# Loading the last eighth of an output projection on half of the DMA engines: a study of one change to a decode-attention kernel

## The chip, the cores and the metric

One core of one Trainium2 chip. The metric is device time of one execution in microseconds; every row of times below is a median over executions. Every experiment was timed in the same rounds, on the same chip, as the kernel before. Different experiments ran on three different chips, so kernels are compared by their ratios to the kernel before, with a 95% interval; a difference of 1% is 2 us here.

## The reference

```python
B, Sq, D = 32, 1, 512            # x
Hq, Hkv, Sk, Dh = 32, 8, 2048, 128
W = max(256, Sk // 4)            # 512: only the last 512 cache rows count
q = (x @ wq) -> [B, Hq, 1, Dh]
scores = q . k[:, :, Sk-W:] * Dh**-0.5;  p = softmax(scores);  o = p . v[:, :, Sk-W:]
return o.reshape(B, 1, Hq*Dh) @ wo       # wo: [4096, 512] bf16
```

The last line is what matters here. Its contraction runs over 4096 rows of `wo`, 4 MB in bf16, which the kernel reads after the caches.

## The kernel before: the parts concerned

`wo` is read in eight eighths of 512 rows. Partition m holds four consecutive rows (4 KB) of each eighth. The contraction therefore needs attention outputs arranged by "row 4m + i", while they lie in `oT_sb` by head and channel; a **selection** moves them: matmuls of `oT_sb` with a 0/1 matrix `band`, then copies into `o_sel`. The first selection takes batches 0 to 27 while the last P·V products still run, the second the last four.

```python
for hg in range(NHG):                                   # NHG = 8, SyncE's queue
    sp.dma_start(wo_sb[:, hg]..., wo[hg*512:(hg+1)*512, :].rearrange("(m i) n -> m (i n)", i=4)
    ).then_inc(sem_wo[hg], 16)
...
def select(b0, b1, dst):                                # TensorE
    pe.wait_ge(dve_oT, b1)
    for i in range(4):
        for hi in range(4):
            ins = pe.matmul(dst(i), lhsT=band[:, i, 96-32*hi:224-32*hi],
                rhs=oT_sb[:, :, b0:b1].rearrange("p (g hi) b -> p hi g b", hi=4)[:, hi], ...)
    ins.then_inc(pe_sel, 1)
...
for it in range(B + PVLAG):                             # PVLAG = 6
    if it < B: transposes(it)
    if 1 <= it <= B: scores(it - 1)
    if it >= PVLAG: pv_matmuls(it - PVLAG)
    if it % 4 == 1 and 5 <= it <= B + 1: pt_transposes((it - 5) // 4)
    if it == SELCUT + PVLAG: ...; select(0, SELCUT, ...)   # SELCUT = 28
select(SELCUT, B, ...)
pe.wait_ge(dve_sel, 2); pe.wait_ge(act_sel, 1)
for hg in range(NHG):                                   # the projection
    pe.wait_ge(sem_wo[hg], 16)
    for i in range(4):
        for c in range(4):
            ins = pe.matmul(KT_ps[:, 2, :].bitcast(F32)[32*c:32*(c+1), 0:128],
                lhsT=o_sel[:, i, hg, :], rhs=wo_sb[:, hg, i, c*128:(c+1)*128], ..., tile_position=(0, 32*c))
```

Of the kernel before, what the change touches and what calls it, by code (L numbers as in the profile page):

```python
# [5 lines left out]
BF16 = mybir.dt.bfloat16  # L6
# [6 lines left out]
def bass_standalone__sliding_block_cached__sampling_kernel(  # L13
# [27 lines left out]
    LEAD = 5  # L41
    PVLAG = 6
    NQUAD = B // 4
    NHG = HQ // 4
    SELCUT = 28

    with ExitStack() as es:  # L47
# [1 line left out]
        ps = lambda name, shape, dt: es.enter_context(nc.psum_tensor(name, shape, dt))  # L49
        sem = lambda name: es.enter_context(nc.semaphore(name))  # L50

        w_sb = sb("w_sb", [P, DKT * HD], BF16)
        wq_sb = w_sb[:, :].rearrange("p (kt n) -> p kt n", kt=DKT)
        wo_sb = w_sb[:, :].rearrange("p (g i n) -> p g i n", g=NHG, i=4)
        K_sb = sb("K_sb", [P, NK, 2, NR, DH], BF16)
        V_sb = sb("V_sb", [P, NV, 2, NR, DH], BF16)
        KT_sb = sb("KT_sb", [P, NKT, 2, NR, G4, NS], BF16)
# [4 lines left out]
        PT_sb = sb("PT_sb", [P, 2, NR, P], BF16)  # L62
        oT_sb = sb("oT_sb", [P, HQ, B], BF16)
        o_sel = sb("o_sel", [P, 4, NHG, B], BF16)
        band = sb("band", [P, 4, 224], BF16)
        xT_sb = sb("xT_sb", [P, DKT, 32], BF16)
        ident = sb("ident", [P, P], BF16)
        perm = sb("perm", [P, G4, NS], BF16)
# [13 lines left out]
        sem_x = sem("sem_x")  # L82
        sem_wq = [sem(f"sem_wq{i}") for i in range(DKT)]
        sem_wo = [sem(f"sem_wo{i}") for i in range(NHG)]
        sem_k = [[sem(f"sem_k{i}_{h}") for h in range(2)] for i in range(NK)]
        sem_v = [sem(f"sem_v{i}") for i in range(NV)]
        sem_out = sem("sem_out")
# [39 lines left out]
        @block.sync  # L127
        def _(sp):
            for kt in range(1, DKT):
                sp.dma_start(wq_sb[:, kt, :], wq[kt * P:(kt + 1) * P, :]).then_inc(sem_wq[kt], 16)  # L130

            def load_k(b):
                if b >= NK:
                    sp.wait_ge(pe_T[3], b - NK + 1)
                for h in range(2):
                    sp.dma_start(  # L136
                        K_sb[:, b % NK, h].rearrange("p r d -> p (r d)"), cache_rows(k_cache, b, h)
                    ).then_inc(sem_k[b % NK][h], 16)

            def load_v(b):  # L140
                if b >= NV:
                    sp.wait_ge(pe_PV, b - NV + 1)
                for h in range(2):
                    sp.dma_start(  # L144
                        V_sb[:, b % NV, h].rearrange("p r d -> p (r d)"), cache_rows(v_cache, b, h)
                    ).then_inc(sem_v[b % NV], 16)

            for b in range(B + LEAD):
                if b < B:
                    load_k(b)  # L150
                if b >= LEAD:
                    load_v(b - LEAD)
            sp.wait_ge(pe_qt, 1)
            for hg in range(NHG):
                sp.dma_start(  # L155
                    wo_sb[:, hg].rearrange("p i n -> p (i n)"),
                    wo[hg * 512:(hg + 1) * 512, :].rearrange("(m i) n -> m (i n)", i=4),
                ).then_inc(sem_wo[hg], 16)
            sp.wait_ge(dve_out, 2)
            sp.wait_ge(act_out, 2)  # L160
            sp.dma_start(
                out.rearrange("b s n -> b (s n)"), out_sb[:, :, :].rearrange("b c n -> b (c n)")
            ).then_inc(sem_out, 16)
            sp.wait_ge(sem_out, 16)

        @block.gpsimd
        def _(pool):
            pool.memset(ident[:, :], 0.0).then_inc(pool_init, 1)
            pool.wait_ge(pool_init, 1)
            pool.affine_select(  # L170
                out=ident[:, :], in_=ident[:, :], compare_op=ALU.not_equal, fill=1.0,
                base=0, pattern=[[-1, P]], channel_multiplier=1,
            ).then_inc(pool_init, 1)
            pool.memset(perm[:, :, :], 0.0).then_inc(pool_perm, 1)
            pool.wait_ge(pool_perm, 1)
            pool.affine_select(
                out=perm[:, :, :], in_=perm[:, :, :], compare_op=ALU.not_equal, fill=1.0,
                base=0, pattern=[[-1, G4], [-G4, NS]], channel_multiplier=1,
            ).then_inc(pool_perm, 1)
            pool.memset(junk[:, :], 0.0).then_inc(pool_init, 1)  # L180
            pool.memset(QBD[:, :, :, :], 0.0).then_inc(pool_init, 1)
            pool.memset(P_ex[:, :, :, :], 0.0).then_inc(pool_ex, 1)
            pool.memset(band[:, :, :], 0.0).then_inc(pool_band, 1)
            pool.wait_ge(pool_band, 1)
            pool.affine_select(
                out=band[:, :, :], in_=band[:, :, :], compare_op=ALU.not_equal, fill=1.0,
                base=384, pattern=[[-1, 4], [-4, 224]], channel_multiplier=1,
            ).then_inc(pool_band, 1)
            pool.wait_ge(pool_init, 4)
            pool.wait_ge(dve_qt, 1)  # L190
            pool.wait_ge(act_qt, 1)
            for b in range(B):
                if b >= NQB:
                    pool.wait_ge(pe_S, b - NQB + 1)
                dst = bass.AP(
                    tensor=QBD, offset=(b % NQB) * G * 32 + score_row(0, b % 4),
                    ap=[[NQB * G * 32, P], [G4 * 32 + 16, 2], [32, G4], [1, REP]],
                )
                src = bass.AP(
                    tensor=QT_sb, offset=b,  # L200
                    ap=[[HQ * B, P], [G4 * REP * B, 2], [REP * B, G4], [B, REP]],
                )
                pool.tensor_copy(dst, src).then_inc(pool_qbd, 1)  # L203

        @block.tensor
        def _(pe):
# [91 lines left out]
                        )  # L298
                ins.then_inc(pe_PV, 1)

            def select(b0, b1, dst):
                pe.wait_ge(dve_oT, b1)
                for i in range(4):
                    for hi in range(4):
                        ins = pe.matmul(
                            dst(i),
                            lhsT=band[:, i, 96 - 32 * hi:224 - 32 * hi],
                            rhs=oT_sb[:, :, b0:b1].rearrange("p (g hi) b -> p hi g b", hi=4)[:, hi],
                            start=(hi == 0), stop=(hi == 3), tile_position=(0, 0), skip_group_check=True,
                        )  # L310
                ins.then_inc(pe_sel, 1)

            for it in range(B + PVLAG):
                if it < B:
                    transposes(it)
                if 1 <= it <= B:
                    scores(it - 1)
                if it >= PVLAG:
                    pv_matmuls(it - PVLAG)
                if it % 4 == 1 and 5 <= it <= B + 1:  # L320
                    pt_transposes((it - 5) // 4)
                if it == SELCUT + PVLAG:
                    pe.wait_ge(pool_band, 2)
                    pe.wait_ge(dve_T, 3 * B)
                    pe.wait_ge(act_T, B)
                    nb = SELCUT
                    select(0, nb, lambda i: KT_ps[:, i // 2, :].bitcast(F32)[
                        :, (i % 2) * NHG * nb:(i % 2 + 1) * NHG * nb])
            nl = B - SELCUT
            select(SELCUT, B, lambda i: KT_ps[:, 3, :].bitcast(F32)[:, i * NHG * nl:(i + 1) * NHG * nl])  # L330
            pe.wait_ge(dve_sel, 2)
            pe.wait_ge(act_sel, 1)
            for hg in range(NHG):
                pe.wait_ge(sem_wo[hg], 16)
                for i in range(4):
                    for c in range(4):
                        ins = pe.matmul(  # L337
                            KT_ps[:, 2, :].bitcast(F32)[32 * c:32 * (c + 1), 0:128],
                            lhsT=o_sel[:, i, hg, :],
                            rhs=wo_sb[:, hg, i, c * 128:(c + 1) * 128],  # L340
                            start=(hg == 0 and i == 0), stop=(hg == NHG - 1 and i == 3),
                            tile_position=(0, 32 * c),
                        )
            ins.then_inc(pe_fin, 1)

        @block.vector
        def _(dve):
# [40 lines left out]
            def sel_evac(bank, i0, ni, b0, b1):  # L388
# [3 lines left out]
                        "p (i g b) -> p i g b", i=ni, g=NHG),  # L392
                )

            def ot_evac(b):
                dve.wait_ge(pe_PV, b + 1)
                dve.tensor_copy(oT_sb[:, :, b], QO_ps[:, 0:HQ]).then_inc(dve_oT, 1)  # L397

            for it in range(B + PVLAG + 1):
# [4 lines left out]
                if it == SELCUT + PVLAG + 1:  # L404
                    dve.wait_ge(pe_sel, 1)
                    dve.tensor_copy(*sel_evac(0, 0, 2, 0, SELCUT)).then_inc(dve_sel, 1)
                if it % 4 == 1 and 5 <= it <= B + 1:
                    softmax_b((it - 5) // 4)
                if it < B:
# [3 lines left out]
                    softmax_a((it - 4) // 4)  # L413
            dve.wait_ge(pe_sel, 2)
            dve.tensor_copy(*sel_evac(3, 0, 4, SELCUT, B)).then_inc(dve_sel, 1)
            dve.wait_ge(pe_fin, 1)
            for c in range(2):
                dve.tensor_copy(  # L418
# [85 lines left out]
```

## Time and profile before

| | before |
|---|---|
| median of 3 executions (range) | 196.53 us (196.02 to 196.56) |
| traffic, mean rate | 75.97 MB, 390 GB/s |
| TensorE / VectorE / ScalarE busy | 74% / 52% / 30% |
| projection can start, ends | 186.78 us, 192.06 us |
| eighth 7 of wo complete | 191.61 us |

The kernel is a stream of transfers with everything else beside it. Two groups of the page concern the end; the columns are busy time, mean ns of one, idle time before, and what ended most of it:

```profile
L337 PE MATMUL KT_ps<-w_sb,o_sel 128*32 128x128 bf16 x128 | 3.8, 289 | 1.9 <-DMA w_sb<-in_wo_dram 1.5
...
w_sb<-in_wo_dram SPq DMA_DIRECT2D x8, 512.0 KB, 15.4
```

The projection costs TensorE 3.8 us and waits for wo; each eighth takes some 15 us from issue to landing. Transfers of this size complete every 1.28 us (the first completions of eighths 0 and 1 are at 177.18 and 178.46), so a dozen are in the queue with it. What stands at the end of the timeline is shown in the prediction.

### The profile page before, as it was taken

To read this page: it belongs to the slowest core of one execution; us is meant where nothing else is said; L and a number is where in the kernel's file an instruction comes from. 1 tells how busy PE (TensorE), PEld (TensorE's weight loads), DVE (VectorE), ACT (ScalarE), POOL (GpSimd) and SP (SyncE) were. 2 spreads that over 40 slices of the span, in tenths; PEclk is the share of its full clock that TensorE was granted. 3 is DMA by queue.
4 is the path that set the end of the run, shared out by engine and by line. 5 is a ranking of instruction groups with operands and counts; after the bars stand their busy time and mean duration, and the time that the engine had idled before them with its cause. 6 is when DMAs were issued, how large, how long until landed. Compare 5 with 4: busy or idle time off the path is not lost.

```text
span 194.7 us, 6153 instructions
## 1 busy us (share of the span) xinstructions
PE 144.0 (74%) x2724; PEld 114.9 (59%) x2724; DVE 102.1 (52%) x190; ACT 57.6 (30%) x70; POOL 15.0 (8%) x45
## 2 busy tenths in 40 slices
PE   0448995877897679749777988779776978937881
PEld 0337773755586567537555667557666667636760
DVE  0005778745684459533944587447943574670211
ACT  3001535622262126213252236204420352213101
POOL 8502000000020001000000000000000000000000
PEclk9999999999699978996999699979998887975558
DMA  5999999999999999999999999999999999999960
GB/s 204 426 420 406 412 405 411 407 410 407 409 407 407 408 408 410 407 407 410 407 407 410 409 407 407 410 406 408 408 406 411 405 410 405 412 405 412 406 251 31
DMA packets 20282, 75.97 MB, mean 390 GB/s; under 512 B 2272, under 2 KB 2336, under 8 KB 19744
## 3 DMA queue, kind: packets, MB, share of 16 engines
q1 hardware_dynamic: 20208, 75.54, 97.2%
q8 instruction: 22, 0.36, 0.8%
q10 hardware_dynamic: 48, 0.03, 0.1%
q14 instruction: 4, 0.03, 0.0%
HBM read 75.53 MB, written 0.03 MB: 388 GB/s over the span
## 4 chain that ended last, share of the span: by engine, by line
SPq 68%; DMA 23%; PE 5%; issue 3%; DVEq 0%; DVE 0%
SPq L144 37%; SPq L136 26%; DMA K_sb<-in_k_cache_dram 15%; DMA w_sb<-in_wo_dram 8%; SPq L155 5%; PE KT_ps L243 4%; SPq L130 1%; PE S_ps L260 1%; PE QO_ps L293 0%; PE KT_ps L337 0%; SPq L118 0%; DVEq L47 0%; DVE out_sb L418 0%
## 5 line engine op out<-in xcount | busy, mean ns | idle before, releaser
L243 PE MATMUL KT_ps<-perm,K_sb 128*128 128x128 bf16 x1024 | 75.2, 235 | 22.4 <-DMA K_sb<-in_k_cache_dram 22.2
L361 DVE COPY KT_sb<-KT_ps 128x1024 bf16<-128x1024 bf16 x96 | 63.6, 689 | 52.2 <-PE KT_ps L243 52.0
L243 PEld LDWEIGHTS KT_ps<-perm,K_sb 128*128 128x128 bf16 x1024 | 65.6, 106 | 30.0 <-DMA K_sb<-in_k_cache_dram 28.4
L435 ACT ACTIVATE KT_sb<-KT_ps 128x1024 bf16<-128x1024 bf16 x32 | 32.8, 1023 | 82.3 <-PE KT_ps L243 82.3
L293 PEld LDWEIGHTS QO_ps<-PT_sb,V_sb 128*128 128x128 bf16 x1024 | 28.3, 97 | 17.8 <-issue 13.5
L293 PE MATMUL QO_ps<-PT_sb,V_sb 128*128 128x16 bf16 x1024 | 31.1, 171 | 3.3 <-DMA V_sb<-in_v_cache_dram 1.3
L383 DVE TENSOR_SCALAR P_ex<-P_f,recip 32x512 bf16<-32x512 f32 x32 | 25.4, 793 | 1.2
L260 PE MATMUL S_ps<-KT_sb,QBD 128*32 128x512 bf16 x256 | 22.2, 428 | 0.0
L453 ACT ACTIVATE PT_sb<-PT_ps 128x1024 bf16<-128x1024 bf16 x16 | 15.5, 1021 | 19.4 <-PE PT_ps L275 19.4
L203 POOL COPY QBD<-QT_sb 128x32 bf16<-128x32 bf16 x32 | 8.5, 279 | 116.1 <-PE S_ps L260 108.1
L275 PE MATMUL PT_ps<-ident,P_ex 128*128 128x128 bf16 x128 | 9.4, 231 | 9.8 <-DVE P_ex L383 9.8
L275 PEld LDWEIGHTS PT_ps<-ident,P_ex 128*128 128x128 bf16 x128 | 7.9, 104 | 10.9 <-DVE P_ex L383 10.8
L397 DVE CAST oT_sb<-QO_ps 128x32 bf16<-128x32 f32 x32 | 9.3, 289 | 7.5 <-PE QO_ps L293 7.5
L221 PE MATMUL PT_ps<-xT_sb,w_sb 128*128 128x32 bf16 x128 | 4.1, 188 | 6.4 <-DMA w_sb<-in_wq_dram 6.4
L367 DVE TENSOR_REDUCE maxv<-S_ps 128x1 f32<-128x512 f32 x8 | 5.5, 691 | 5.4 <-PE S_ps L260 5.4
L221 PEld LDWEIGHTS PT_ps<-xT_sb,w_sb 128*128 128x128 bf16 x128 | 3.7, 104 | 6.8 <-DMA w_sb<-in_wq_dram 4.6
L443 ACT ACTIVATE P_f<-S_ps,negmax 128x512 f32<-128x512 f32 x8 | 5.5, 687 | 6.3 <-DVE negmax L369 6.3
L260 PEld LDWEIGHTS S_ps<-KT_sb,QBD 128*32 128x32 bf16 x256 | 3.9, 96 | 3.9 <-issue 1.4
L353 DVE CAST QT_sb<-PT_ps 128x512 bf16<-128x512 f32 x1 | 0.7, 691 | 10.3 <-PE PT_ps L221 10.3
L337 PE MATMUL KT_ps<-w_sb,o_sel 128*32 128x128 bf16 x128 | 3.8, 289 | 1.9 <-DMA w_sb<-in_wo_dram 1.5
L337 PEld LDWEIGHTS KT_ps<-w_sb,o_sel 128*32 128x32 bf16 x128 | 2.9, 131 | 2.7 <-DMA w_sb<-in_wo_dram 2.2
L427 ACT ACTIVATE QT_sb<-PT_ps 128x512 bf16<-128x512 f32 x1 | 0.6, 597 | 12.0 <-PE PT_ps L221 12.0
(28 smaller groups left out, 22.4 us busy)
## 6 DMA issues: line engine op xcount, KB each, us to landing
K_sb<-in_k_cache_dram SPq DMA_DIRECT2D x64, 512.0 KB, 15.6
V_sb<-in_v_cache_dram SPq DMA_DIRECT2D x64, 512.0 KB, 15.4
w_sb<-in_wq_dram SPq DMA_DIRECT2D x4, 1024.0 KB, 8.3
w_sb<-in_wo_dram SPq DMA_DIRECT2D x8, 512.0 KB, 15.4
x_sb<-in_x_dram ACTq DMA_DIRECT2D x1, 32.0 KB, 2.9
out_dram<-out_sb SPq DMA_DIRECT2D x1, 32.0 KB, 1.5
```

Of the source, the lines that this page charges most:

```text
L136: sp.dma_start(K_sb[:, b % NK, h].rearrange("p r d -> p (r d)"), cache_rows(k_cache, b, h)).then_inc(sem_k[b % NK][h], 16)
L144: sp.dma_start(V_sb[:, b % NV, h].rearrange("p r d -> p (r d)"), cache_rows(v_cache, b, h)).then_inc(sem_v[b % NV], 16)
L155: sp.dma_start(wo_sb[:, hg].rearrange("p i n -> p (i n)"), wo[hg * 512:(hg + 1) * 512, :].rearrange("(m i) n -> m (i n)", i=4),).then_inc( ...
L243: ins = pe.matmul(KT_ps[:, t, i * 128:(i + 1) * 128], lhsT=K_sb[:, b % NK, h, 8 * (t % 2) + i, :], rhs=perm[:, :, :], start=True, stop=Tru ...
L260: ins = pe.matmul(S_ps[32 * c:32 * c + 32, :], lhsT=QBD[:, b % NQB, g, :], rhs=KT_sb[:, b % NKT, h, :, c, :], start=(j == 0 and h == 0), s ...
L275: ins = pe.matmul(PT_ps[:, r // 8, (r % 8) * 128:(r % 8 + 1) * 128], lhsT=P_ex[:, r, :, :].rearrange("p s g -> p (s g)"), rhs=ident[:, :], ...
L293: ins = pe.matmul(QO_ps[:, 16 * h:16 * h + 16], lhsT=V_sb[:, b % NV, h, r, :], rhs=PT_sb[:, q % 2, r, :].rearrange("p (c n) -> p c n", c=G ...
L361: dve.tensor_copy(KT_sb[:, b % NKT, t // 2, 8 * (t % 2):8 * (t % 2) + 8, :, :], KT_ps[:, t, :]).then_inc(dve_T, 1)
L383: dve.tensor_scalar(P_ex[rows, :, :, c], P_f32[rows, :].rearrange("p (r s) -> p r s", r=NR), recip[rows, q:q + 1], None, op0=ALU.mult,).th ...
L397: dve.tensor_copy(oT_sb[:, :, b], QO_ps[:, 0:HQ]).then_inc(dve_oT, 1)
L435: act.activation(KT_sb[:, b % NKT, 1, 8:16, :, :], KT_ps[:, 3, :], ACTF.Copy).then_inc(act_T, 1)
L453: act.activation(PT_sb[:, q % 2, 8 * i:8 * i + 8, :].rearrange("p r n -> p (r n)"), PT_ps[:, i, :], ACTF.Copy,).then_inc(act_PT, 1)
```

## The change

Intent: in the end phase half of the DMA engines run dry early (of the sixteen completions of eighth 7, eight are in by 188.40 us, the last at 191.61). Give the last eighth of `wo` to engines that are done first: as eight transfers of eight rows, with 8 KB rows in partitions 0 to 63. That layout puts eight rows of wo on a partition instead of four, so it needs its own selection (`band8`, 64 columns of weights) and a contraction over 64 rows with eight steps.

```diff
-    NHG = HQ // 4
+    NHG = HQ // 4 - 1;  NTP = 64;  NTI = 8
+            for half in range(2):
+                for r in range(4):
+                    rows = slice(32 * half + r, 32 * half + 32, 4)
+                    sp.dma_start(wt_sb[rows]..., wo[NHG*512:, :].rearrange("(m i) n -> m (i n)", i=NTI)[rows]
+                    ).then_inc(sem_wt, 16)
...                                     # GpSimd: memset and affine_select of band8
-            def select(b0, b1, dst):
+            def select(b0, b1, dst, dst_t):
...
+                for i in range(NTI):
+                    for hi in range(4):
+                        ins = pe.matmul(dst_t(i), lhsT=band8[:, i, 48 - 16*hi:112 - 16*hi],
+                            rhs=oT_sb[:, 4 * NHG + hi, b0:b1], ...)
...                                     # VectorE: one more copy (into t_sel) after each selection
+            pe.wait_ge(sem_wt, 128)
+            for i in range(NTI):
+                for c in range(4):
+                    ins = pe.matmul(KT_ps[...], lhsT=t_sel[:, i, :], rhs=wt_sb[:, i, c*128:(c+1)*128],
+                        start=False, stop=(i == NTI - 1), tile_position=(0, 32*c))
```

## The prediction

> **What bounds the kernel now.** I read the page first: its slices, then its chain that ended last.

> ```profile
> DMA  5999999999999999999999999999999999999960
> GB/s 204 426 420 406 412 405 411 407 410 407 409 407 407 408 408 410 407 407 410 407 407 410 409 407 407 410 406 408 408 406 411 405 410 405 412 405 412 406 251 31
> ...
> SPq L144 37%; SPq L136 26%; DMA K_sb<-in_k_cache_dram 15%; DMA w_sb<-in_wo_dram 8%; SPq L155 5%; PE KT_ps L243 4%; SPq L130 1%; PE S_ps L260 1%; PE QO_ps L293 0%; PE KT_ps L337 0%; SPq L118 0%; DVEq L47 0%; DVE out_sb L418 0%
> ```

> The DMA engines are busy in 37 of 40 slices at some 408 GB/s, and the chain is nearly all transfers and their issue: 75 MB of traffic sets the time, and no engine's arithmetic does. The change moves the same bytes, so only the last ten microseconds can give or take. There the rate is 251, then 31 GB/s: in the last two slices most DMA engines have run out while a few still work. The timeline of the end:

> ```profile
> 178.59 3.15 PE L305 MATMUL KT_ps<-oT_sb,band 128*128 128x224 bf16 x16
> ...
> 185.79 0.61 PE L305 MATMUL KT_ps<-oT_sb,band 128*128 128x32 bf16 x16 [0.39 <-DVE oT_sb L397]
> 186.44 0.29 DVE L415 CAST o_sel<-KT_ps 128x128 bf16<-128x128 f32 x1 [0.70 <-PE KT_ps L305]
> 186.78 2.06 PEld L337 LDWEIGHTS KT_ps<-w_sb,o_sel 128*32 128x32 bf16 x80 [0.49 <-DVE o_sel L415]
> 186.78 3.00 PE L337 MATMUL KT_ps<-w_sb,o_sel 128*32 128x128 bf16 x96 [0.38 <-DVE o_sel L415]
> ...
> 190.41 0.41 PE L337 MATMUL KT_ps<-w_sb,o_sel 128*32 128x128 bf16 x16 [0.63 <-DMA w_sb<-in_wo_dram]
> ...
> 191.66 0.41 PE L337 MATMUL KT_ps<-w_sb,o_sel 128*32 128x128 bf16 x16 [0.83 <-DMA w_sb<-in_wo_dram]
> ```

> TensorE is ready for the output projection at 186.78, catches up with the first five eighths of wo near 189, and then waits for eighths 5, 6 and 7, which are complete at 189.12, 190.37 and 191.61. The kernel ends when eighth 7 has landed and its 16 matmuls are done. The slack is small: 2.4 us from TensorE being ready to its first wait.

> Why do the eighths land late? Each 128-row transfer leaves sixteen completions in the trace, one per DMA engine. For eighth 6 the first is at 184.82, the eighth at 187.20, the ninth at 187.91, the last at 190.37; for eighth 7: 186.09, 188.40, 189.15, 191.61. In the first K transfer the spread was 0.94 us. The offsets stay constant to 0.1 us over long stretches, then one completion steps back by about 1.5 us each time a 16 KB packet of another queue passes:

> ```profile
> q8 instruction: 22, 0.36, 0.8%
> ```

> The sequence of steps repeats after eight: the ninth and tenth packet hit completions that the first and second had already moved back, so I read that only eight of the sixteen engines carry these packets, and the other eight finish some 3 us earlier. I cannot see an engine's number in the trace.

> [...] The trace before has nothing but transfers over 16 engines (128 or 32 rows)[...]. [...] the P·V matmuls (128 columns of weights, 16 moving) follow each other every 26.7 ns[...]. Nothing before has 64 columns on one position.

> **The change, part by part.**

> Transfers. Removed: eighth 7 as one transfer, 8 packets of 4 KB (159 ns each) on each of 16 engines. Added: 8 transfers of 8 rows of 8 KB[...]. An 8 KB packet takes 309 ns (the wq rows), so 8 take 2.45 us, against 1.25 us for eighth 7. Issue: the shortest issues in the trace take 0.36 to 0.6 us, back-pressured ones 1.08; eight of them from 176.64 end between 180 and 185.5, early enough. If engines 0 to 7 are the eight that carry no instruction packets, they start the tail between 184.82 and 187.20 and finish by 187.20 + 2.45 = 189.65. Then the last landing is eighth 6 at 190.37 instead of eighth 7 at 191.61: 1.24 us earlier.

> The end of TensorE. From 190.41 the program still has 16 matmuls for eighth 6 and then 32 for the tail (64 rows deep, but the number of matmuls doubles from 16 to 32). Four column tiles take 55 ns at full clock and 107 ns at half clock, so 48 matmuls take 0.66 us (full) or 1.28 us (half), plus 0.22 us until the last one drains. The windows table says which clock holds:

> ```profile
> 178.50:185.80 7.30, 6.13 (x122) 5.28 (x119) 1.81 (x5) 0.54 (x1) 0.00 (x0) 0.50 1.03 407
> 185.80:190.00 4.20, 3.54 (x112) 2.90 (x112) 0.29 (x1) 0.00 (x0) 0.00 (x0) 0.50 0.53 212
> 190.00:192.20 2.20, 0.81 (x32) 0.47 (x32) 0.08 (x1) 0.09 (x1) 0.00 (x0) 0.98 0.13 45
> ```

> The seventh figure after the length (PEclk) is 0.50 until 190 and then 0.98. At full clock the end of TensorE would be 190.41 + 0.66 + 0.22 = 191.29 against 192.06 before: a gain of 0.77 us if nothing else moved.

> The added selection. TensorE works alone through 178.6 to 186.8, so what is added there delays the projection. First selection: 16 matmuls shrink from 224 to 196 columns, at 1.2 columns per ns: 16 × 28 / 1.2 = −0.37 us. Added are 32 with 64 columns of weights and 28 moving. [...] if they go like 128 columns do here, 27 ns, 0.86 us. Second selection: 16 matmuls from 32 to 28 columns, −0.05 us; 32 added with 4 moving columns, again 1.71 or 0.86 us. VectorE has one more copy after each: the 128x448 copy took 0.62 us and the 128x128 one 0.29, so about 0.39 us for 224 columns and 0.2 for 32; the first delays the next evacuation only slightly, the second lies wholly in the path. Sum to the start of the projection: (1.71 − 0.37 + 0.1) + (1.71 − 0.05) + 0.25 = 3.4 us, so about 190.2; with 27 ns each 1.7 us, about 188.5. The slack of 2.4 us is thus overdrawn in the first case: 144 matmuls from 190.2 at full clock take 2.0 + 0.22 us and end at 192.4, 0.35 us later than before. In the second case the data still set the end and 191.3 to 191.5 holds: −0.65 us. GpSimd's extra memset and select (0.84 and 0.95 us for the same 896 columns) end near 9.5, well ahead of 15.47 where it is next needed: nothing.

> **The rivals.** (1) The eight engines are the wrong ones, those with the instruction packets. Then the slowest reaches the end of eighth 6 at 190.37 and needs 2.45 us more: 192.85, plus 32 matmuls and drain, 0.66 us: 193.5, or +1.4 us. For it: the trace has no numbers of engines. [...] I give it 0.25. (2) The selection takes the place of the transfer: right engines, but TensorE is the bound at the end, +0.35 us; if the clock stays at half to the end, 144 matmuls take 3.85 us and it is +2 us. For it: the half clock[...]. Against it: the pitch of 26.7 ns at 128 columns. I give it 0.45, of which 0.1 for half clock. (3) The intended gain: right engines, short selection, −0.65 us, 0.30. (4) All 16 engines share the eight-row transfers after all; the landing is then as before, and the selection alone costs up to 0.4 us. This lies within the others.

> **Range and chances.** 0.25 × 1.4 + 0.35 × 0.35 + 0.10 × 2 + 0.30 × (−0.65) = +0.48 us; executions of the kernel before differ by 0.5 us. From 196.53 I predict 196.9 us, and 195.7 to 198.6 holds all but the worst mixtures. Two per cent is 3.9 us, more than any of these makes: within 2% 0.96, slower 0.03 (weights slower still at half clock together with wrong engines), faster 0.01.

> **What would show the steps right or wrong.** The tail's semaphore should show 64 increments right at issue and 64 with data[...]. The tail's last landing near 189.6 says right engines, near 193 wrong ones. The last landing of wo on the whole should be 190.4 in the first case. The mean pitch of the 32 added selection matmuls decides between 53 and 27 ns. The idle time of the tail's matmuls says what bounds: none before them means TensorE, one put down to the wo transfer means DMA. The prediction would be wrong if the steady stage changed its rate, or if issuing eight transfers held up earlier ones.

## The result, and the profile after

| | before | after |
|---|---|---|
| median (range), 4 executions each | 196.41 us (196.02 to 196.56) | 198.38 us (197.82 to 198.63) |
| ratio | | 1.0099, interval 1.0073 to 1.0126 |
| first selection starts | 178.59 us | 177.90 us |
| projection starts | 186.78 us | 189.53 us |
| last landing of wo | 191.61 us | 190.89 us |
| projection ends | 192.06 us | 193.66 us |

A ratio here is the mean time of one kernel's executions over that of the other's of the same rounds, so not quite the ratio of the medians. The change is 1% slower: within 2%, but clear of noise. The two lines of the page that answer to those of before:

```profile
DMA  5999999999999999999999999999999999999930
GB/s 214 426 415 409 408 407 407 411 407 411 405 412 405 410 408 406 409 409 409 407 409 405 410 407 407 412 405 407 410 407 410 407 411 405 407 410 407 392 153 7
...
SPq 54%; DMA 24%; PE 14%; DVE 3%; issue 3%; ACT 1%; DVEq 0%; ACTq 0%
```

The last two slices move 153 and 7 GB/s instead of 251 and 31, but a slice is a fortieth of the span, so in the longer run these two begin some 1.5 us later. In the same stretch, 189.5 to 193.4, it is 13 GB/s instead of 40 (last figures of the windows below): the transfers do end somewhat earlier. In the chain that ended last TensorE now has 14% and VectorE 3%, where TensorE had 5%. The end in the timeline:

```profile
177.90 2.77 PE L324 MATMUL KT_ps<-oT_sb,band 128*128 128x196 bf16 x16
...
180.60 1.89 PE L332 MATMUL KT_ps<-oT_sb,band 128*64 128x28 bf16 x32
...
187.20 1.87 PE L332 MATMUL KT_ps<-oT_sb,band 128*64 128x4 bf16 x32
189.11 0.27 DVE L462 CAST o_sel<-KT_ps 128x112 bf16<-128x112 f32 x1 [2.50 <-PE KT_ps L332]
189.30 0.17 DVE L463 CAST t_sel<-KT_ps 64x32 bf16<-64x32 f32 x1
189.53 2.91 PEld L367 LDWEIGHTS KT_ps<-w_sb,o_sel 128*32 128x32 bf16 x112 [0.54 <-DVE t_sel L463]
189.53 3.18 PE L367 MATMUL KT_ps<-w_sb,o_sel 128*32 128x128 bf16 x112 [0.46 <-DVE t_sel L463]
192.63 0.77 PEld L377 LDWEIGHTS KT_ps<-w_sb,t_sel 64*32 64x32 bf16 x32 [0.20 <-issue]
```

Read the brackets. Before, the projection's matmuls waited for `in_wo_dram`; now none does. The first 112 run without a break from 189.53, released by VectorE's copy of the added selection, and the 32 of the tail follow though the tail had been complete since 190.89. TensorE is the bound of this execution. And its clock, in two windows:

```profile
184.50:189.50 5.00, 3.79 (x94) 3.48 (x90) 0.96 (x4) 0.00 (x0) 0.00 (x0) 0.50 0.71 286
189.50:193.40 3.90, 3.87 (x144) 3.68 (x144) 0.00 (x0) 0.00 (x0) 0.00 (x0) 0.50 0.04 13
```

The second window of the kernel before, for comparison:

```profile
189.50:193.40 3.90, 1.10 (x44) 0.48 (x36) 0.56 (x2) 0.54 (x2) 0.00 (x0) 0.93 0.11 40
```

Two things must be kept out of the comparison of these two profiles. The execution of the change ran about 0.7 us ahead of the other: its first selection starts 0.69 us earlier, and eighth 6 of wo, which both kernels load alike, landed at 189.65 instead of 190.37. And some of the loss lies outside the profile: the time of an execution exceeds its span by 2.07 us in the median over all 51 executions of kernels that build `band8`, and by 1.83 us over 50 of those that don't. This quarter of a microsecond is part of the ratio of every kernel below that builds `band8`; no run shows where it goes.

**The engines.** The tail's semaphore moves 72 times in the trace: eight steps between 177.12 and 181.87, one 0.4 to 0.5 us after most of the eight issues end, and 64 with data. The tail's 32 matmuls wait for a count of 128 and ran, so with 64 from the data each of the eight early steps counted eight: each eight-row transfer had eight engines at work, and the other half of its count came soon after its issue. The 64 form chains with steps of 0.31 us, one 8 KB packet each. The chains start where an engine finished eighth 6: six of them between 185.1 and 187.3, but two at 188.2 and 188.4. So two of the eight engines that carry the tail were late ones, and they end it at 190.64 and 190.89. These eight are called the lower eight below, and the prediction and the expected texts give them the numbers 0 to 7; these are names only, for the trace has no engine numbers.

### The profile page after: what moved, and what is told of

It reads as the page before. It is cut to its first block, busy times and chain, and to the rows that moved or that the text cites.

```text
span 196.3 us, 6325 instructions
## 1 busy us (share of the span) xinstructions
PE 147.7 (75%) x2804; PEld 119.7 (61%) x2804; DVE 102.2 (52%) x192; ACT 57.6 (29%) x70; POOL 16.5 (8%) x47
## 4 chain that ended last, share of the span: by engine, by line
SPq 54%; DMA 24%; PE 14%; DVE 3%; issue 3%; ACT 1%; DVEq 0%; ACTq 0%
SPq L150 29%; SPq L142 24%; DMA K_sb<-in_k_cache_dram 24%; PE KT_ps L262 4%; PE QO_ps L312 3%; PE KT_ps L332 2%; PE KT_ps L324 2%; PE KT_ps L367 2%; DVE P_ex L423 2%; PE S_ps L279 1%; ACT PT_sb L501 1%; SPq L136 1%; PE PT_ps L294 1%; PE KT_ps L377 1%; DVE oT_sb L443 0%
## 5 line engine op out<-in xcount | busy, mean ns | idle before, releaser
L332 PEld LDWEIGHTS KT_ps<-oT_sb,band 128*64 128x64 bf16 x64 | 3.6, 156 | 0.3 <-issue 0.3
L332 PE MATMUL KT_ps<-oT_sb,band 128*64 128x28 bf16 (+1 forms) x64 | 3.8, 203 | 0.0
```

The source lines that it names most:

```text
L332: ins = pe.matmul(dst_t(i), lhsT=band8[:, i, 48 - 16 * hi:112 - 16 * hi], rhs=oT_sb[:, 4 * NHG + hi, b0:b1], start=(hi == 0), stop=(hi == ...
```

## The experiments

Theory A: the loss is TensorE's, through the added selection in its serial end, under the half clock. Theory B: the loss is in the transfers, through their number or their late landing. The first two runs take each of these parts alone; the others alter one detail, of the change or of the kernel before.

### The selection alone

The kernel before with eight whole eighths of wo, plus the added selection, whose result nobody reads.

```diff
  (before, NHG = 8, loads as they were)
+ band8, t_sel; 32 selection matmuls of 64 weight columns in each select(); two VectorE copies
```

> The kernel before with its eight whole eighths of wo, plus the added selection of the change (64 matmuls of 64 weight columns and two VectorE copies whose result nobody reads). Theory A (TensorE pays: added selection in its serial end, under the half clock): the projection starts 3.3 to 3.9 us later than the 186.78 us of before, about 190.3, and its 128 matmuls at half clock (26.7 ns each) end near 193.9; time about 198.2 us, as slow as the change or slower. Theory B (the eight-row transfers or their late landing pay): no such transfers here, so the time stays that of the kernel before, 196.4.

Measured: 198.75 us (197.09 to 199.35, 7 executions), ratio 1.0117 (1.0099 to 1.0134). The selection by itself costs as much as the whole change (the intervals overlap), though the transfers are those of before. Its profiled execution was the fastest of the seven, at 197.09: TensorE's clock was granted in full for 3.4 us at 180.2, so the first 32 added matmuls took 1.18 us instead of 1.89, and the projection started at 188.79:

```profile
188.79 3.60 PE L358 MATMUL KT_ps<-w_sb,o_sel 128*32 128x128 bf16 x128 [0.47 <-DVE t_sel L444]
```

Still no wait for wo: 128 matmuls without a break to 192.4. I had expected the start at 190.3 for half clock throughout; that spell, and an execution 0.6 us ahead of the other (first selection at 177.95), account for the difference. Theory A holds for this part.

### The transfers alone

The change without its selection; the tail's contraction reads rows of `o_sel` instead of `t_sel`, so the result is wrong.

```diff
- 32 matmuls with band8 in select(); the two copies into t_sel
- lhsT=t_sel[:, i, :]
+ lhsT=o_sel[0:NTP, i % 4, i // 4, :]
```

> The change without its added selection: the eight 8-row transfers and the 64-row contraction stay, but the contraction reads rows of the main selection instead (wrong result on purpose). Theory A: TensorE is ready near 186.4 us, waits for wo and ends about 0.7 us after the tail's last landing at 190.9: 191.6 against 192.06 before, so 195.9 us, slightly faster than before. Theory B: as slow as the change, 198.4 us.

Measured: 198.28 us (197.16 to 198.66, 6 executions), ratio 1.0065 (1.004 to 1.009). Theory A had said 195.9. It fails as the only cause. The times fall into two groups, 197.2 (two) and 198.3 to 198.7 (four), and the profile is of the second:

```profile
190.49 0.62 PE L359 MATMUL KT_ps<-w_sb,o_sel 128*32 128x128 bf16 x16 [0.67 <-DMA w_sb<-in_wo_dram]
192.94 0.77 PEld L369 LDWEIGHTS KT_ps<-w_sb,o_sel 64*32 64x32 bf16 x32 [2.10 <-DMA w_sb<-in_wo_dram]
```

TensorE waits 2.10 us for the tail, which lands at 192.90, later than eighth 7 did before (191.61). The two late chains of completions start where engines finished eighth 6 at about 189.8 and 190.4, among the last of all, and then need eight packets more. In the change's profile the two started at 188.2 and 188.4. So there is a second limit, and it moves from execution to execution. An execution in which the tail lands late, after 192 us, is called bad below, one in which it lands near 191 us good.

### Wide selection weights

```diff
- band8 = sb("band8", [P, NTI, 112], BF16);  lhsT=band8[:, i, 48 - 16*hi:112 - 16*hi]
+ band8 = sb("band8", [P, NTI, 176], BF16);  lhsT=band8[:, i, 48 - 16*hi:176 - 16*hi]
```

> The change with its selection weights widened from 64 to 128 columns by columns of zeros (right result). If 64 columns are slow [...], the 64 matmuls take 27 ns each instead of 55.6: 0.9 us less twice, the projection starts near 187.7 us instead of 189.53, and the time falls by about 1.8 us to 196.6. If the matmuls' pitch is set by something else, nothing changes: 198.4 us.

Measured: 197.88 us (196.85 to 198.52, 6 executions), ratio 1.0055 (1.0029 to 1.0081), right result. The second 32 added matmuls, both kernels at half clock:

```profile
186.43 0.99 PE L332 MATMUL KT_ps<-oT_sb,band 128*128 128x4 bf16 x32
187.46 0.28 DVE L462 CAST o_sel<-KT_ps 128x112 bf16<-128x112 f32 x1 [1.53 <-PE KT_ps L332]
```

0.99 us against the change's 1.87: twice as many weight columns, half the time. The projection starts at 187.88, as expected. The ratio fell by 0.4%, not by the 0.9% that 1.8 us would be: TensorE then stood still for 0.90 us in mid-projection, released by no semaphore that the profile shows, and in other executions the tail's landing may have bounded the end. The pitch is settled, the gain is only partial.

```profile
190.34 1.89 PE L367 MATMUL KT_ps<-w_sb,o_sel 128*32 128x128 bf16 x63 [0.90 <-issue]
```

The stop has a likely cause in the traces. It comes after the 50th weight load of the projection here and in the runs "Four engines", "One transfer" and "The first selection in TensorE's wait", and after the 32nd in "Warm and wide together", where 18 idle matmuls come first: always at the same place of TensorE's program. In all five it ends 2.5 to 2.6 us after the start of the last packet but one of the instruction queue q8 (187.87 here). The change gets to this place 3.0 us after that packet and does not stop. So a TensorE that gets ahead seems to run into a block of instructions that has not arrived; no run moved the place of the block, so this is a reading and not shown.

### Eight engines, old layout

Eighth 7 in its 4 KB rows and 128 partitions, by sixteen transfers of eight neighbouring rows; no selection added.

```diff
+ for r in range(0, P, 8):
+     sp.dma_start(wo_sb[r:r + 8, hg]..., wo[hg*512:(hg+1)*512, :]...[r:r + 8]).then_inc(sem_wo[hg], 16)
```

> The kernel before with eighth 7 loaded in its old layout of 4 KB rows, by sixteen transfers of eight rows, [...]; no added selection, no added matmuls. Theory A: eighth 7 lands at about 190.9 us instead of 191.61, TensorE ends 0.45 us later, time about 195.8 us, 0.3% faster than before. If many small transfers cost something themselves (theory B), the landing is later than 191.6 and the time above 196.4.

Measured: 198.58 us (198.35 to 200.37, 6 executions), ratio 1.012 (1.0087 to 1.0153). The 195.8 us of theory A failed, and the outcome was that of theory B. The profiled execution is one of the two slowest, at 200.08, and its eighth 7 landed at 195.03. From 185 us on the packets of all engines stretched, from 159 ns to a median of 227 at 186 us, and eighth 6 landed at 191.83 instead of 190.4. Why they stretched, this run does not show. The run "Rows four partitions apart" below keeps the sixteen transfers and changes only which rows each of them takes.

### Four engines

```diff
- for half in range(2): for r in range(4): rows = slice(32*half + r, 32*half + 32, 4)
+ for quarter in range(4): for r in range(4): rows = slice(16*quarter + r, 16*quarter + 16, 4)
```

> The change with its tail loaded by sixteen transfers of four rows, to see which engines carry the tail: if a four-row transfer runs on engines 0 to 3 alone, the tail's 64 completions with data form four chains of sixteen steps of 0.31 us, and each chain starts where one engine finished eighth 6. In the change's trace two of the eight chains started late (engines that also fetch instructions). Theory A1: those two are among engines 4 to 7, so all four chains start early and the tail lands at 186.1 + 4.9 = 191.0 us at the latest. Theory A2: they are among 0 to 3, and the tail lands between 193 and 195.5 us, by the phase of the fetching. Time: A1 as the change, 198.4 us (TensorE-bound); A2 198.5 to 200 us.

Measured: 198.52 us (4 executions), ratio 1.0113 (1.0092 to 1.0134), as A1 had it. The semaphore moved 80 times, 16 at issue and 64 with data, so four engines took part. The tail landed at 192.40, between the two figures expected; 16 packets back from there is 187.4, so no chain had started as late as 188.9, where the late engines of that run finished eighth 6. If the two late engines of the lower eight are the same in every execution, and these four are among the eight (neither was shown), then they are not among the four. TensorE was not ready before 192.89, so the landing did not bound this run.

### One transfer

```diff
+ sp.dma_start(wt_sb..., wo[NHG*512:, :].rearrange("(m i) n -> m (i n)", i=NTI)).then_inc(sem_wt, 16)
```

> The change with its tail as one transfer of 64 rows, [...], selection and contraction kept. If the added selection bounds the end, the time is that of the change or a little less, 198 to 198.5 us, whatever the transfer does. If the choice of engines were what the change loses by, the time would fall to 196.5 us. A landing later than 191.7 us would mean that two engines writing one half of the partitions get in each other's way.

Measured: 198.97 us (198.89 to 199.03, 4 executions), ratio 1.0125 (1.0112 to 1.0138); above the 198 to 198.5 expected. The tail landed at 193.12, later than the 191.7 that the expected text had named as the sign of engines in each other's way, just as TensorE was ready for it (193.07, after a stop of 0.82 us). The transfers of 128 and of 32 rows in the trace of before left sixteen completions each; from that I estimate that this one of 64 rows ran on all 16 engines too, twice as many as in the change for the same partitions 0 to 63. Its 8 KB packets took 622 ns in the mean at 185 us instead of 309: two to one. Eighth 3, issued before it, already landed 2.07 us after eighth 2 (186.87 after 184.80) where 1.25 is usual. So the change's confinement to eight engines is not idle: with the tail as one transfer over the same partitions, a packet took twice as long.

### A warm clock

The change plus 18 idle matmuls of 512 columns into free PSUM, where TensorE waits: four after P·V of batch 26, nine before and five after the last transposes of P.

```diff
+ def warm(dst, n):
+     for _ in range(n):
+         pe.matmul(dst, lhsT=ident[:, :], rhs=K_sb[:, (B-1) % NK, 0, 0:4, :], start=True, stop=True, ...)
```

> The change plus 18 idle matmuls of 512 columns, put where TensorE waits between 168 and 178 us, to keep its granted clock up. If the half clock between 173 us and the end is what makes the added selection dear, the clock stays near 1.0, the two selections and the projection take about 4 us less, TensorE becomes ready before the data, and the time is set by the tail's landing: 196.0 to 198.3 us by the phase of the fetching, 197 in the mean. If the clock does not follow the work, the time is that of the change, 198.4 us, or worse by what the idle matmuls delay.

Measured: 196.46 us (196.23 to 196.81, 4 executions), ratio 0.9999 (0.9984 to 1.0014). The whole loss is gone in these four executions, by adding work. The windows:

```profile
173.00:178.50 5.50, 4.70 (x68) 3.21 (x67) 1.59 (x4) 1.94 (x2) 0.00 (x0) 1.00 1.03 410
178.50:184.50 6.00, 4.83 (x147) 4.36 (x145) 1.74 (x5) 0.50 (x1) 0.00 (x0) 1.00 1.02 408
184.50:189.50 5.00, 4.54 (x139) 4.42 (x135) 0.36 (x2) 0.00 (x0) 0.00 (x0) 0.51 0.73 291
```

PEclk, 0.50 in the change over the same stretches, is 1.00 in the first two. It did not stay there, as I had expected: from 184.6 on it is 0.50 again, so the second selection (1.87 us for its added 32, as in the change) and nearly all of the projection still run at half clock. What shrinks is the part before:

```profile
179.04 1.18 PE L332 MATMUL KT_ps<-oT_sb,band 128*64 128x28 bf16 x32
...
187.05 3.51 PE L382 MATMUL KT_ps<-w_sb,o_sel 128*32 128x128 bf16 x112 [0.46 <-DVE t_sel L478]
189.93 0.35 PEld L382 LDWEIGHTS KT_ps<-w_sb,o_sel 128*32 128x32 bf16 x16 [0.40 <-DMA w_sb<-in_wo_dram]
190.68 0.76 PEld L392 LDWEIGHTS KT_ps<-w_sb,t_sel 64*32 64x32 bf16 x32 [0.40 <-DMA w_sb<-in_wo_dram]
```

The projection starts at 187.05 instead of 189.53, waits for wo again, and the tail's matmuls are released by its landing at 190.64. They end 1.0 us later, at 191.6, so 0.4 us before those of the kernel before; the medians differ by 0.1. All four executions seem to be good ones by their times; of the twelve of the two other kernels with a tail and idle matmuls, below, three took over 198 us and seem bad. So part of this result may be luck.

### Rows four partitions apart

The old-layout experiment, with a transfer's rows four partitions apart.

```diff
- for r in range(0, P, 8): rows r:r + 8
+ for r in [32*b + r for b in range(4) for r in range(4)]: rows = slice(r, r + 29, 4)
```

> The earlier experiment with 4 KB rows in the old layout [...], whose packets stretched from 159 to 227 ns and whose eighths 4 to 6 landed up to 1.4 us late. Here the eight rows of a transfer are four partitions apart, as in the change, instead of neighbours. [...] the packets of the first half (partitions 0 to 63) take 159 ns again, eighths 4 to 6 land on time (190.4), and only those for partitions 64 to 127, [...] may stretch; the time is 196 to 197.5 us. If packets stretch just as much, it is the many small transfers, and the time stays 198.6 us.

Measured: 198.3 us (197.57 to 199.31, 6 executions), ratio 1.0096 (1.0074 to 1.0117). The packets did as expected: at 185 us the median was 159 ns and the mean 160, where neighbouring rows had stretched them to 227 at 186 us; at 187 and 188 the median was 306 and 304 ns, twice that. The first eight transfers, for partitions 0 to 63, are 8 packets of 159 ns for an engine, 1.3 us, so by estimate the long ones fall to the rows of partitions 64 to 127; the trace does not show which engines write these. But the time was outside my range: I had not counted that eighth 6 would be late as well, and it landed at 192.5 instead of 190.4. Both layouts in which eight-row transfers reach over all 128 partitions lose (ratios 1.012 and 1.0096).

### The first selection in TensorE's wait

The wide-weights kernel with SELCUT 27, its first selection ahead of the last transposes of P.

```diff
- SELCUT = 28
+ SELCUT = 27
-   if it % 4 == 1 and 5 <= it <= B + 1: pt_transposes((it - 5) // 4)
    if it == SELCUT + PVLAG: ...; select(0, SELCUT, ...)
+   if it % 4 == 1 and 5 <= it <= B + 1: pt_transposes((it - 5) // 4)
```

> The change with wide selection weights, and with its first selection moved: it takes batches 0 to 26 instead of 0 to 27 and stands before the last transposes of P, where TensorE waits some 2 us for VectorE; so real work fills the wait. The selection leaves the serial end: the projection should start at 185 to 186 us instead of 189.53, with the clock up for longer, and the end be set by the tail's landing alone: 191.3 us (195.8 us in all) [...], up to 193.5 us (198.0) [...]. If the selection were not what holds TensorE, the projection would start as late as in the change.

Measured: 198.08 us (198.04 to 198.22, 4 executions), ratio 1.0091 (1.0078 to 1.0104). The projection started at 185.92, as expected, and the end was the second of my two cases:

```profile
189.99 0.62 PE L367 MATMUL KT_ps<-w_sb,o_sel 128*32 128x128 bf16 x16 [0.62 <-DMA w_sb<-in_wo_dram]
192.47 1.04 PE L377 MATMUL KT_ps<-w_sb,t_sel 64*32 64x128 bf16 x32 [1.86 <-DMA w_sb<-in_wo_dram]
```

TensorE, ready 3.6 us earlier than in the change, waits 1.86 us for a tail that lands at 192.42. Its two late chains start at 189.8 and 189.9.

### Control: the kernel before, warm

```diff
  (before, with the same 18 idle matmuls)
```

> Control: the kernel before with the same 18 idle matmuls. It waits for eighth 7 to land at 191.6 us whatever TensorE does, so a higher clock should gain nothing but the last 16 matmuls: 196.4 to 196.6 us, no difference. If it gains 0.5% or more, the idle matmuls help by another way than TensorE's end, and the reading of the warmed change falls.

Measured: 196.37 us (196.35 to 196.4, 5 executions), ratio 1.0003 (0.9991 to 1.0015). No gain, as expected, and its last stretch, 189.5 to 193.4, even ran at 0.50 instead of 0.93: the kernel before does not care for TensorE's clock. So there is no sign that the idle matmuls help by another way than TensorE's serial end; whether in the change they also move the instruction packets, and with them the landing, this control cannot say.

### Transfers alone, warm

```diff
  (transfers alone, with the same 18 idle matmuls; wrong result on purpose)
```

> Transfers only (no added selection, wrong result on purpose) with the 18 idle matmuls. Its end was set by the tail's landing (192.90 us) and not by TensorE's clock; so the idle matmuls should gain at most the difference of the last 32 matmuls at full clock, 0.4 us: 197.2 to 198.2 us, or two groups of runs, about 196.5 and 198, by where the instruction fetching stands. If it falls to 196.4 in all runs, the landing was not what held it.

Measured: 196.81 us (196.47 to 198.01, 6 executions), ratio 1.0033 (1.0011 to 1.0055). Two groups again, five at 196.5 to 196.9 and one at 198.0. The profile is of the first group: the tail landed at 191.01, and its 32 matmuls followed at once:

```profile
190.35 0.62 PE L374 MATMUL KT_ps<-w_sb,o_sel 128*32 128x128 bf16 x16 [0.62 <-DMA w_sb<-in_wo_dram]
191.06 1.04 PE L384 MATMUL KT_ps<-w_sb,o_sel 64*32 64x128 bf16 x32
```

Cold, four of six were slow; warm, one of six. So few executions cannot tell whether the idle matmuls shift the state of the fetching or chance did.

### Warm and wide together

```diff
  (wide selection weights, with the 18 idle matmuls)
```

> The change with the 18 idle matmuls and the wide selection weights together. With the idle matmuls alone TensorE and the landing were level (190.68 against 190.64 us), so 1.0 to 1.8 us less selection can gain only what the wait for eighth 6 and the tail leave: 0 to 0.4 us, 196.1 to 196.5 us. A gain of 1 us or more would say that TensorE still was the bound there.

Measured: 196.79 us (196.53 to 198.36, 6 executions), ratio 1.0048 (1.0018 to 1.0078): four at 196.5 to 196.8, two at 198.3 and 198.4. The 196.1 to 196.5 expected was missed; the reading that TensorE is no longer the bound stands. The profile is of a bad one: TensorE ready at 185.79, tail landed at 192.59. Where TensorE is out of the way, or level with the landing as in the first row, the landing alone sorts the executions that were profiled:

| kernel | tail lands | time of that execution |
|---|---|---|
| warm change | 190.64 us | 196.32 us |
| transfers alone, warm | 191.01 us | 196.79 us |
| first selection early | 192.42 us | 198.22 us |
| warm and wide | 192.59 us | 198.36 us |
| transfers alone | 192.90 us | 198.66 us |

In every row the time is 5.7 to 5.8 us after the landing. No version found beats the kernel before.

## Why the prediction was right or wrong

The measured 198.38 us lies in the range, 0.2 us below its upper end, and 1.5 us above the central 196.9 (the prediction's own sum, 196.53 + 0.48, is 197.0). Point by point:

- **Eight engines for an eight-row transfer: right.** In the change eight steps came at issue and 64 completions with data, eight for each transfer; with four rows sixteen and 64, four for each. Before the run this was an assumption: all transfers in the trace of before have 128 or 32 rows and sixteen completions.
- **Cost of the selection: right, in part by luck.** From the start of the first selection to that of the projection it is 11.63 us (189.53 − 177.90) against 8.19 us before: 3.44 us more, where the sum said 3.4. Its first 32 weight loads begin between 180.602 and 182.228, so 1.626 us / 31 = 52.5 ns apart, against the 53 ns (1.71 us for 32) of the sum's dearer case (the 55.6 ns in the expectations is 1.78 us / 32, with the length of the last load in it). The luck is that the dearer case was an assumption, with no load of 64 columns in the trace of before to show it, and that it fits the half clock (0.50) of this stretch: with 1.00 granted the same loads lay 31.4 ns apart in the warm run (179.041 to 180.015). The 1.2 columns per ns of the sum are the half clock's too: 224 columns followed each other every 187 ns in the trace of before. The wide weights, 128 columns, halved the time of the second 32 (0.99 us against 1.87).
- **The clock at the end: the step that failed.** I took full clock after 190 from the windows of before and gave 2.2 us for the 144 matmuls, draining included. The half clock went on to 193.5, and they took 4.13 us (189.53 to 193.66). This term was 1.9 us too small, and the pitch accounts for it: 36 steps of 107 ns instead of 56. I had the case as part of rival 2 with 0.10 and "+2 us"; that is what happened: 1.6 us between the two profiled ends, 2.0 us in the medians. No run gave the projection itself the full clock: in the warm run it ran at 0.51 too. What that run shows, with its ratio of 0.9999 and a control that gained nothing, is that TensorE's serial end was the bound of the change and that a higher clock in its first part, up to 184.6, took the loss away.
- **The tail's landing: the path was wrong, the mechanism half right.** I had eighth 6 landing last, at 190.37, with the tail before it. In every profile the tail landed after eighth 6. I had the tail on the eight engines without instruction packets, done by 189.65; that it would be these was an assumption, which no trace showed. Two of its eight were late ones, and the tail ended at 190.89; in other runs, where two of them had been delayed last, at 192.4 to 192.9. In these two profiles wo is complete 0.7 us earlier and not 1.24, but by as much the execution was ahead: counted from the landing of eighth 6 the last eighth takes 1.24 us in both. Counted so, the tail on eight engines took 0.70 to 1.24 us in the four good profiles (the change's own has the 1.24) and 2.45 to 2.50 us in the three bad ones. That the instruction packets are what delays them was read from the steps of completions in the trace of before; no run took the packets away, so it stays a reading. Which engines carry them, and what sets the state at the start of an execution, stay open.
- **Rivals.** Rival 2 (the selection takes the place of the transfer) was the truth of the profiled execution. Rival 1 (wrong engines) is true in part and by execution: it alone explains the slow group once TensorE is out of the way. The two limits lie within 0.4 us of each other in the bad state (TensorE's end at 193.66; a landing at 192.90 ends the projection near 194.0), which fits with either one, taken away alone, giving back only part.

The intended gain in landing was at most about half a microsecond, in good executions: 0.70 us after eighth 6 instead of 1.24. From it go 16 more matmuls behind the last landing: the warm change's 32 end 1.0 us after the landing, the 16 of before 0.45 us after it, so nothing is left. That the warm change's profile ends 0.4 us before that of the kernel before is no more than the 0.5 us by which its eighth 6 was early; the medians differ by 0.1 us.

## What to carry to other kernels

Work added to a serial end is to be priced at the clock that the end will have once the work is there (0.50 here), not at the one that the old trace shows (0.98); where TensorE idles before such an end, even useless matmuls in that idle time can pay: here they gave back what the added work had cost (ratio 0.9999), and no more. Moving bytes to engines that are done first pays only for engines that are done first in every execution: look at the completions of several runs before choosing (here the tail followed eighth 6 by 0.70 to 2.50 us), and count them from a transfer that the change leaves alone. And when a transfer is cut up or laid out anew, look at how long its packets take: those of the change kept their 309 ns, while in the three runs with another layout they took 1.4 to 2.0 times as long (medians of 227 and 306 ns against 159, a mean of 622 against 309).
